# Gate matmuls of the last 1024 tokens split into an upper and a lower half of the array's rows

## The chip, the core and the metric

The kernel runs on one core of a Trainium2 chip. A core has a matrix engine (TensorE, "PE" in the profile, with its weight loads listed apart as "PEld"), a vector engine (VectorE, "DVE"), a scalar engine (ScalarE, "ACT"), a general one (GpSimd, "POOL") and a queue engine that issues transfers (SyncE, "SP"). Matrix products are written to PSUM, which has eight banks of 512 float32 columns by 128 partitions; VectorE and ScalarE carry results from there to SBUF, the working memory.

The metric is the time of one execution in microseconds of the device. Lower is better. Several executions are timed, and one further execution is profiled.

## What is computed

Windowed attention with summarised keys, followed by a gated network without a nonlinearity. Cut to what matters here (batch 4, 8 heads, 768 positions, head size 64; so 3072 tokens of 512 features; 1024 hidden features):

```python
def reference(**kwargs):
    attn_out = _attn_ref(**attn_kwargs)            # (4, 8, 768, 64)
    x = attn_out.transpose(0, 2, 1, 3).reshape(3072, 512)
    a = x @ w1                                     # 512 x 1024
    b = x @ w2                                     # 512 x 1024
    h = a * b @ w3                                 # 1024 x 1024
    return h @ w_out                               # 1024 x 512
```

## The kernel before

**Stages.** The kernel first folds `w3 @ w_out` into one 1024 x 512 matrix while the first attention steps run. Tokens then go in units of U = 512. The first two units (1024 tokens) go through plain products (`gate`, `project`, recorded at the helper's line L123). The other 2048 tokens go in two groups, n = 1 and n = 2, of two units each, through a scheme that forms a 2 x 2 block product out of seven products instead of eight: `gates(n, whole)` for `x @ w1` and `x @ w2`, then `project_fast(n, whole)` for the output. Attention steps for later tokens run between pieces of these products until about 385 us; n = 2 has the stretch behind that to itself, after the rest of `project_fast(1, ...)`.

**Numbers.** Each factor is kept as a high and a low part in the type fp32r, so a product is three matmuls: high by high, low by high, high by low.

**`lanes` (matmul at L708).** This helper runs the seven products for both callers. It takes one PSUM bank for each lane from the list `tags`; for each product k in the order of `o.ids`, for each lane i and each of `steps` chunks of 128 input rows it issues the three matmuls of 128 x 128 weights against 128 x 512 values into `banks[i]`. In `gates` there are 4 lanes of 128 gate features and KH = 2 steps, so a lane of one product is 6 matmuls. `gates` calls it twice, for r = 0 and r = 1, each with its half of the hidden features: 2 x 7 x 4 x 6 = 336 matmuls for n = 2, and as many for n = 1.

**Running sums in PSUM.** Products of one group go on adding into the same bank: `start` is set only on the first product of a group. For n = 2 the order is `EARLY_SUM`: products 0, 4, 5, 6 are one group, 2, 3 the next, 1 alone. After each product the bank's sum so far is carried out, and the next product's matmuls of that lane write to the same bank only after that.

**`add_up` (L726, L728).** It carries a lane out to one of the four SBUF tiles of the lane (`tmp`, `tmp`, `hr`, `hr`). Where the table `o.adds[k]` names no second summand, ScalarE copies (L726: products 0, 4, 5, 6 for n = 2); otherwise VectorE adds the bank to a tile (L728: products 2, 3, 1). After products 3 and 1 VectorE multiplies the finished `x @ w1` by `x @ w2` (L785).

**What follows.** `Whole.moving` prepares the values of `project_fast`: differences of the `hr` tiles (VectorE, L615), a copy to the high part (ScalarE, L619) and the low part (VectorE, L119, tile `hT`).

**Order on the engines.** The order on TensorE and GpSimd is that of the program. The order on VectorE and ScalarE is made at build time by a planner that goes by priorities and its own idea of durations; `tc.high_priority(offset=SOONER)` puts the evacuations of `lanes` 400 places ahead. Once made, each engine works through its queue in that order. PSUM tiles are shared by tag: "mm" has 2 banks, "tp" 2, "sc" 4. The gates use the two "mm" and the two "tp" banks; the four "sc" banks belong to attention (scores, transposes and outputs).

Of the kernel before, what the change touches and what calls it, by code (L numbers as in the profile page):

```python
# [15 lines left out]
ALU = mybir.AluOpType  # L16
# [3 lines left out]
P = 128  # L20
# [50 lines left out]
def attention_moe(ctx, tc, qG, kW, kT, vP, vW, vB, mask, w1, w2, w3T, wo, out, outT):  # L71
    nc = tc.nc
# [3 lines left out]
    U = TOKENS  # L76
# [5 lines left out]
    D = P // 2  # L82
# [8 lines left out]
    KH = NC // 2  # L91
# [596 lines left out]
    def flow_in(n):  # L688


        while flow and len(ready) < n and (not flow[0][0] or flow[0][0] in stored):
            t = sb.tile([P, 2, 512], F32R, name="ws", tag="x", bufs=6)
            flow.pop(0)[1](t)
            ready.append(t)

    def lanes(n, o, weights_of, moving_of, steps, evacuated, tags, between=None):

        banks = [ps.tile([P, 512], F32, name="ln", tag=tag, bufs=bufs) for tag, bufs in tags]
        for at, k in enumerate(o.ids):
            stationary_of = yield from weights_of(at, k)  # L700
            for i in range(n):
                for c in range(steps):
                    if between and c % KH == 0:
                        between(at, i * steps // KH + c // KH)
                    a, m = [stationary_of(i, c, w) for w in range(2)], moving_of(k, c)
                    terms = [(a[0], m[0]), (a[1], m[0]), (a[0], m[1])]
                    for j, (x, y) in enumerate(terms):
                        nc.tensor.matmul(  # L708
                            banks[i][:, :U],
                            lhsT=x,  # L710
                            rhs=y,
                            start=c + j == 0 and k in o.first,
                            stop=c == steps - 1 and j == 2 and k in o.last,
                            skip_group_check=True,
                        )
                    if c < steps - 1:
                        yield 3 * U
                with tc.high_priority(offset=SOONER):
                    evacuated(at, k, i, banks[i][:, :U])
                yield 3 * U  # L720

    def add_up(o, k, parts, got):

        to, more = o.adds[k]
        if more is None:
            nc.scalar.copy(parts[to], got)  # L726
        else:
            nc.vector.tensor_tensor(parts[to], got, parts[more], ALU.add)  # L728

    xT, raws, kept, hT, tasks, background = {}, {}, {}, {}, [], []  # L730

# [2 lines left out]
    def moving_x(n, at):  # L734

        o = ORDERS[n]
        k = o.ids[at]

        def start():
            while any(kept.get((n, half), 0) < NC for half in range(2 if k > 1 else 1)):  # L740
                yield -1
            t = sb.tile([P, 2, KH, U], F32R, name="xT", tag="w12", bufs=8)
            works = []
            for c in range(KH):
                b = [[raws[n, half][c + i * KH] if (n, half) in raws else None for half in range(2)] for i in range(2)]
                works.append(moving(o, k, b, (t[:, 0, c], t[:, 1, c]), o.before.get(k, (k,))))
            yield from staggered(works)
            xT[n, k] = t

        tasks.append(start())  # L750

    def gates_flow(n):
        flow.extend((2 <= k < NK - 1 and ("w%d" % (2 * r + i), k), lambda t, k=k, r=r, i=i: nc.sync.dma_start(t.bitcast(F32), wS[k][2 * r + i])) for r in range(NF // 4) for k in ORDERS[n].ids for i in range(2))

    def gates(n, whole):


        o = ORDERS[n]
        for r in range(NF // 4):
            if r == NF // 4 - 1:  # L760
                flow.extend(output_flow(k, c) for k in LATE.ids for c in range(2))
                if n + 1 < NSU:
                    gates_flow(n + 1)

            def weights_of(at, k):
                while (n, k) not in xT:
                    yield -1
                flow_in(6)
                while len(ready) < 2:
                    yield -1  # L770
                    flow_in(6)
                if n > 1 and r == 0 and at + 2 < NK:
                    moving_x(n, at + 2)
                two = [ready.pop(0), ready.pop(0)]
                return lambda i, c, w: two[i // 2][:, w, c * FQ + i % 2 * P : c * FQ + i % 2 * P + P]

            parts = []

            def evacuated(at, k, i, got):
                if at == 0:  # L780
                    parts.append(whole.parts(i))
                add_up(o, k, parts[i], got)
                if k in o.done:
                    half, a, b = o.done[k]
                    nc.vector.tensor_tensor(parts[i][a], parts[i][a], parts[i][b], ALU.mult)  # L785
                if r == NF // 4 - 1:
                    whole.after(at, i)

            tags = [("mm", 2), ("mm", 2), ("tp", 2), ("tp", 2)]
            yield from lanes(4, o, weights_of, lambda k, c: [xT[n, k][:, w, c] for w in range(2)], KH, evacuated, tags)  # L790

    def temporary():
        t = sb.tile([P, 2, U], F32, name="tmp", tag="wp", bufs=NF)
# [42 lines left out]
    def output_flow(k, c):  # L836
        if 2 <= k < NK - 1:
            return ("p%d" % c, k), lambda t: nc.sync.dma_start(t.bitcast(F32), pS[k][c])

        def load(t):  # L840
            for j in range(2):
                i = 2 * c + j + (0 if k == 0 else NF // 2)
                at = DH if k == NK - 1 else 0
                nc.sync.dma_start(t.bitcast(F32)[:, :, j * DH : (j + 1) * DH], pW[i][:, :, at : at + DH])

        return None, load

    def project_fast(n, whole):
# [18 lines left out]
        def evacuated(at, k, i, got):  # L867
            if at == 0:
                parts.append((*temporary(), *temporary()))
            add_up(LATE, k, parts[i], got)  # L870
            done = {1: (0, 0, 2), 4: (0, 1, 3), 5: (1, 1, 1), 6: (1, 0, 0)}
            if k in done:
                half, u, t = done[k]
                rows, cols = half * DH + i * P, (n - 1) * 2 * U + u * U
                nc.sync.dma_start(outT[rows : rows + P, cols : cols + U], parts[i][t])

        tags = [("mm", 2), ("mm", 2)]
        yield from lanes(2, LATE, weights_of, lambda k, c: hT[n, k][c], NF // 2, evacuated, tags, between)

    def spill_weights(q):  # L880
# [42 lines left out]
    def network():  # L923
        for u in range(2):
            hs = []
            for fs in ([0, 1],) if u else ([0], [1]):
                yield from gate(fs, xs[u], hs, u == 1)
            for f in range(2, NF):
                yield from gate([f], xs[u], hs, u == 1)
            yield from project(u, (0, 1), hs, (range(NF - 1), range(NF - 1, NF)))  # L930
            for t in range(2, NBLK):
                yield from project(u, (t,), hs, (range(NF),))
        for n in range(1, NSU):
            whole = Whole(n)
            yield from gates(n, whole)
            yield from project_fast(n, whole)
# [215 lines left out]
    with tc.manual_schedule(engines={engines.SP, engines.PE}):  # L1152
        start_loads(0)
        active, pairs, t = [], [], [-1]
        while units or active or pairs or delayed or WORK or t[0] <= FIRST[-1]:
# [20 lines left out]
            if t[0] in FIRST[: NPAIR + 1]:  # L1176
                n = FIRST.index(t[0])
# [167 lines left out]
```

## Time and profile before

| what | value |
|---|---|
| median of 3 runs | 515.07 us (512.62 to 517.27) |
| profiled execution, its own time | 512.96 us |
| span of the profiled execution, first to last instruction | 511.2 us |
| granted TensorE clock, mean | 0.993 |
| TensorE busy | 487.7 us (95% of the span) |
| VectorE busy | 365.1 us (71%) |
| ScalarE busy | 314.2 us (61%) |

The profile is one execution taken by the hardware profiler. In a row of a timeline the first number is the start in microseconds from the start of the span, the second how long the row lasts from the first start to the last end, then engine, line, operation, what is written and read, the form, and how many instructions the row holds; in brackets stands idle time of the engine before it and what ended it. In a row of a group the numbers behind the bar are the busy time in us and the mean length of one instruction in ns, then the engine's idle time before these instructions and what ended most of it. Matmuls are pipelined, so their records overlap; the distance from start to start tells their rate. The chain of waits is followed back from the last instruction of the program: at each step to what released it.

### The profile page before, as it was taken

Reading aid. Unit: us, or ns where it says so; the run is one execution under the profiler, and the core shown is the slowest. Engines: PE = TensorE matmul, PEld = TensorE weight load, DVE = VectorE, ACT = ScalarE, POOL = GpSimd, SP = SyncE. Lnnn points to the kernel's source line nnn. Section 1 sums busy time; section 2 is a strip of 40 time slices with the busy share of each in tenths; the row PEclk is TensorE's granted clock in tenths of the full one; section 3 lists DMA queues with packets and bytes.
Section 4 is the critical chain, followed back from the end, with each engine's and each line's share of the span. In section 5 each row is a group of like instructions: output and inputs, shape, how many; then the busy total and the mean of one; then the engine's idle time right before and its main releaser. Section 6 shows DMA issues by size and latency. Waiting matters only on the chain.

```text
span 511.2 us, 10373 instructions
## 1 busy us (share of the span) xinstructions
PE 487.7 (95%) x3744; PEld 392.1 (77%) x3744; DVE 365.1 (71%) x883; ACT 314.2 (61%) x879; POOL 46.9 (9%) x86
## 2 busy tenths in 40 slices
PE   0989987999999999999999999999999999999996
PEld 0767766888887877777777887877787888888885
DVE  4979987688833598985459795899978029129972
ACT  5588964468635788878797677657875421423710
POOL 1024433011201210000000000000000000000000
PEclk9999997999999999999999999999999999999999
DMA  8996699999299989889987999998677755655762
GB/s 342 414 375 244 259 305 321 359 398 412 82 286 306 272 283 281 260 254 339 334 302 251 311 311 333 338 327 252 210 247 247 240 179 192 206 174 197 211 200 85
DMA packets 57220, 139.82 MB, mean 274 GB/s; under 512 B 6224, under 2 KB 19024, under 8 KB 54608
## 3 DMA queue, kind: packets, MB, share of 16 engines
q1 hardware_dynamic: 54864, 134.95, 77.5%
q0 software_dynamic: 1152, 2.10, 2.5%
q10 hardware_dynamic: 1152, 2.10, 1.1%
q8 instruction: 30, 0.49, 0.4%
q14 instruction: 22, 0.18, 0.1%
HBM read 106.42 MB, written 32.70 MB: 272 GB/s over the span
## 4 chain that ended last, share of the span: by engine, by line
PE 83%; DVE 5%; DMA 5%; ACT 5%; issue 1%; SPq 0%; ACTq 0%
PE ln L708 46%; PE mm L123 27%; PE po L433 5%; PE sc L355 4%; PE tp L413 2%; DMA rows<-in_vP_dram 2%; ACT sm L383 2%; DVE wf L186 2%; DMA v<-in_vW_dram 2%; DMA wraw<-in_wo_dram 1%; ACT wf L174 1%; ACT w L200 1%; DVE wf L183 1%; DVE w L119 1%; DVE ks L246 1%
## 5 line engine op out<-in xcount | busy, mean ns | idle before, releaser
L708 PE MATMUL ln<-xT,ws 128*128 128x512 f32 x672 | 157.1, 392 | 0.0
L708 PEld LDWEIGHTS ln<-xT,ws 128*128 128x128 f32 x672 | 125.0, 188 | 27.6 <-issue 0.8
L123 PE MATMUL mm<-x,w 128*128 128x512 f32 x384 | 92.5, 399 | 0.0
L123 PEld LDWEIGHTS mm<-x,w 128*128 128x128 f32 x384 | 72.7, 192 | 16.4 <-issue 0.8
L383 ACT ACTIVATE sm<-sm,mx 128x120 f32<-128x120 f32 x192 | 73.9, 389 | 9.3 <-DVE mx L369 9.3
L708 PE MATMUL ln<-hT,ws 128*128 128x512 f32 x336 | 78.3, 392 | 0.0
L728 DVE TENSOR_TENSOR tmp<-ln,tmp 128x512 f32<-128x512 f32 x52 | 35.8, 688 | 56.3 <-PE ln L708 42.1
L708 PEld LDWEIGHTS ln<-hT,ws 128*128 128x128 f32 x336 | 62.6, 188 | 13.4 <-issue 0.2
L123 PE MATMUL mm<-w,w 128*128 128x512 f32 x192 | 50.2, 414 | 14.3 <-ACT w L200 11.9
L619 ACT CAST hT<-hr 128x512 fp32r<-128x512 f32 x56 | 32.1, 622 | 42.6 <-DVE hr L785 35.4
L123 PEld LDWEIGHTS mm<-w,w 128*128 128x128 f32 x192 | 36.8, 197 | 24.7 <-ACT w L200 12.1
L369 DVE CUSTOM_DVE_ANT_0 sm<-sc,mask_sb 128x120 f32<-128x120 f32 x192 | 42.2, 276 | 15.1 <-PE sc L355 15.0
L123 PE MATMUL mm<-wp,h 128*128 128x512 f32 x192 | 46.3, 395 | 0.0
L393 ACT ACTIVATE sm<-sm,mx 128x120 f32<-128x120 f32 x128 | 38.9, 387 | 6.1 <-DVE mx L389 6.1
L123 PEld LDWEIGHTS mm<-wp,h 128*128 128x128 f32 x192 | 35.4, 188 | 8.0 <-issue 0.5
L119 DVE TENSOR_TENSOR hT<-hr,hT 128x512 fp32r<-128x512 f32 x56 | 35.5, 684 | 3.2 <-ACT hT L619 3.0
L383 ACT ACTIVATION_READ_ACCUMULATOR sm<-sm,mx 128x1 f32 x192 | 36.8, 192 | 0.0
L342 POOL COPY k<-ks 128x96 f32<-128x96 f32 (+1 forms) x32 | 12.9, 412 | 218.3 <-DMA k<-in_kW_dram 178.4
L433 PEld LDWEIGHTS po<-pt,v 120*64 120x64 f32 x768 | 25.2, 141 | 9.2 <-issue 5.0
L200 ACT CAST w<-wf 128x1024 fp32r<-128x1024 f32 (+1 forms) x22 | 21.3, 967 | 14.0 <-DVE wf L186 14.0
L433 PE MATMUL po<-pt,v 120*64 120x64 f32 x768 | 28.7, 229 | 1.1 <-DMA v<-in_vW_dram 0.6
L174 ACT ACTIVATE wf<-wraw 128x1024 f32<-128x1024 f32 (+1 forms) x22 | 23.1, 1056 | 8.0 <-DMA wraw<-in_wo_dram 3.6
(60 smaller groups left out, 548.5 us busy)
## 6 DMA issues: line engine op xcount, KB each, us to landing
ws<-wS SPq DMA_DIRECT2D x56, 512.0 KB
wraw<-in_w3T_dram SPq DMA_DIRECT2D x8, 1024.0 KB
wraw<-in_w_dram SPq DMA_DIRECT2D x8, 1024.0 KB
wS<-sp SPq DMA_DIRECT2D x16, 512.0 KB
ws<-pS SPq DMA_DIRECT2D x16, 512.0 KB
k<-in_kW_dram SPq DMA_DIRECT2D x20, 368.0 KB
raw<-in_kT_dram SPq DMA_DIRECT2D x16, 392.0 KB
q<-in_qG_dram SPq DMA_DIRECT2D x24, 256.0 KB
```

Source lines behind the costliest of these rows:

```text
L119: eng.tensor_tensor(dst, src, hi.bitcast(F32), ALU.subtract)
L123: nc.tensor.matmul(acc, lhsT=a, rhs=b, start=first and i == 0, stop=last and i == len(terms) - 1)
L174: nc.scalar.activation(f[:, some], words[:, some, 1].bitcast(F32), AF.Prelu, scale=2.0**-112, alpha=-(2.0**32),)
L200: nc.scalar.copy(t[:, 0, some], f[:, some])
L355: nc.tensor.matmul(sc[h][64 * g : 64 * g + 64, i * KR : (i + 1) * KR], lhsT=q[rows, i * P + 64 * g : i * P + 64 * g + 64], rhs=k[rows, i, ...
L369: nc.vector.tensor_tensor_reduce(out=sm[:, j], in0=sc[h][:, i * KR : (i + 1) * KR], in1=mask_sb[:, 0 if blk == 0 else 2 if blk == BLOCKS - ...
L383: nc.scalar.activation(sm[:, j], sm[:, j], AF.Exp, bias=mx[:, 0, j : j + 1], scale=-1.0, accum_out=mx[:, 1, j : j + 1])
L393: nc.scalar.activation(sm[:, j], sm[:, j], AF.Copy, scale=mx[:, 2, j : j + 1])
L433: nc.tensor.matmul(po[cols, at : at + 64], lhsT=v[:KR, g, i, cols], rhs=pt[g][:, (h * NBLK + i) * 64 : (h * NBLK + i + 1) * 64], start=Tru ...
L619: nc.scalar.copy(dst[0], src)
L708: nc.tensor.matmul(banks[i][:, :U], lhsT=x, rhs=y, start=c + j == 0 and k in o.first, stop=c == steps - 1 and j == 2 and k in o.last, skip ...
L728: nc.vector.tensor_tensor(parts[to], got, parts[more], ALU.add)
```

## The change

For n = 2, `gates` gives `lanes` eight banks instead of four: the four "sc" banks besides. Where a product is "apart", every matmul over 128 rows is issued as two matmuls over 64 rows, the upper half of weights and values into `banks[i]` and the lower half into `banks[i + 4]`, one behind the other. The sum over the 128 rows is then not complete in one bank: `add_up` gets both banks and carries the first out as before (copy or add), then adds the second with VectorE. All products of n = 2 are apart but products 1, 2 and 3 of the second pass (r = 1). The gates of n = 1 and both calls of `project_fast` have as many banks as lanes and stay as they are.

```diff
-    def lanes(n, o, weights_of, moving_of, steps, evacuated, tags, between=None):
+    def lanes(n, o, weights_of, moving_of, steps, evacuated, tags, between=None, whole=lambda k, i: False):
...
                     a, m = [stationary_of(i, c, w) for w in range(2)], moving_of(k, c)
                     terms = [(a[0], m[0]), (a[1], m[0]), (a[0], m[1])]
+                    apart = len(banks) > n and not whole(k, i)
                     for j, (x, y) in enumerate(terms):
-                        nc.tensor.matmul(
-                            banks[i][:, :U],
-                            lhsT=x,
-                            rhs=y,
-                            start=c + j == 0 and k in o.first,
-                            stop=c == steps - 1 and j == 2 and k in o.last,
-                            skip_group_check=True,
-                        )
+                        for h in range(2 if apart else 1):
+                            rows = slice(h * D, (h + 1) * D) if apart else slice(P)
+                            nc.tensor.matmul(
+                                banks[i + h * n][:, :U],
+                                lhsT=x[rows],
+                                rhs=y[rows],
+                                start=c + j == 0 and k in o.first,
+                                stop=c == steps - 1 and j == 2 and k in o.last,
+                                skip_group_check=True,
+                            )
...
                 with tc.high_priority(offset=SOONER):
-                    evacuated(at, k, i, banks[i][:, :U])
+                    evacuated(at, k, i, [bank[:, :U] for bank in banks[i :: n][: 1 + apart]])
...
         to, more = o.adds[k]
-        if more is None:
-            nc.scalar.copy(parts[to], got)
-        else:
-            nc.vector.tensor_tensor(parts[to], got, parts[more], ALU.add)
+        for some in got:
+            if more is None:
+                nc.scalar.copy(parts[to], some)
+            else:
+                nc.vector.tensor_tensor(parts[to], some, parts[more], ALU.add)
+            more = to
...
-            tags = [("mm", 2), ("mm", 2), ("tp", 2), ("tp", 2)]
-            yield from lanes(4, o, weights_of, lambda k, c: [xT[n, k][:, w, c] for w in range(2)], KH, evacuated, tags)
+            tags = [("mm", 2), ("mm", 2), ("tp", 2), ("tp", 2)] + ([("sc", 4)] * 4 if n >= 2 else [])
+            yield from lanes(4, o, weights_of, lambda k, c: [xT[n, k][:, w, c] for w in range(2)], KH, evacuated, tags, None, lambda k, i, r=r: r == 1 and k in (1, 2, 3))
```

## The prediction

> **What bounds the kernel now.** I read the page first, then the chain of waits, then the busy time by stage, then single stretches of TensorE and VectorE.
>
> ```profile
> span 511.2 us, 10373 instructions
> PE 487.7 (95%) x3744; PEld 392.1 (77%) x3744; DVE 365.1 (71%) x883; ACT 314.2 (61%) x879; POOL 46.9 (9%) x86
> PE ln L708 46%; PE mm L123 27%; PE po L433 5%; PE sc L355 4%; PE tp L413 2%; DMA rows<-in_vP_dram 2%; ACT sm L383 2%; DVE wf L186 2%; DMA v<-in_vW_dram 2%; DMA wraw<-in_wo_dram 1%; ACT wf L174 1%; ACT w L200 1%; DVE wf L183 1%; DVE w L119 1%; DVE ks L246 1%
> ...
> 384.49 1.08 PE po L433 x32
> 385.57 121.46 PE ln L708 x534
> 507.06 0.69 DVE tmp L728
> ```
>
> The last rows are the end of the chain, in order of time: from 385.6 to 507.1 us TensorE alone sets the time, in one unbroken run of L708 matmuls. The gates of the last 1024 tokens lie in it:
>
> ```profile
> 392.44 38.65 PE L708 MATMUL ln<-xT,ws 128*128 128x512 f32 x169
> 430.70 38.24 PE L708 MATMUL ln<-xT,ws 128*128 128x512 f32 x168
> 429.79 6.51 PE L708 MATMUL ln<-xT,ws 128*128 128x512 f32 x28
> L708 PEld LDWEIGHTS ln<-xT,ws 128*128 128x128 f32 x672 | 125.0, 188 | 27.6 <-issue 0.8 <-DVE tmp L728 0.3 <-ACT tmp L726 0.2
> L708 PE MATMUL ln<-xT,ws 128*128 128x512 f32 x672 | 157.1, 392 | 0.0
> ```
>
> The timeline rows show the passes r = 0 (392.4 to 430.7) and r = 1 (to 468.8). A matmul record lasts 0.39 us, but they overlap: (6.51 - 0.39) / 27 = 226.7 ns from start to start. Each pass is 7 products of 4 lanes of 6 matmuls, so a lane takes 1.36 us. Whatever is saved or lost here, up to the last matmul, is saved or lost in the total.
>
> Stage by stage (columns: stretch, its length, then busy time of PE, PEld, DVE, ACT, POOL with instructions, granted clock, DMA share, GB/s):
>
> ```profile
> 392.40:414.20 21.80, 21.80 (x97) 17.80 (x97) 3.15 (x6) 9.35 (x17) 0.00 (x0) 1.00 0.70 223
> 414.20:430.60 16.40, 16.40 (x74) 13.59 (x73) 11.66 (x18) 1.49 (x3) 0.00 (x0) 1.00 0.58 195
> 430.60:452.40 21.80, 21.80 (x98) 18.06 (x97) 6.39 (x11) 10.09 (x18) 0.00 (x0) 1.00 0.56 193
> 452.40:468.80 16.40, 16.40 (x74) 13.55 (x74) 11.97 (x19) 1.21 (x2) 0.00 (x0) 1.00 0.59 195
> ```
>
> The products come in the order 0, 4, 5, 6, 2, 3, 1. In the first and third rows (0, 4, 5, 6) ScalarE copies each lane out and VectorE is nearly free. In the second and fourth (2, 3, 1) VectorE adds each lane and multiplies after products 3 and 1: 11.66 of 16.4 us are taken. DMA (0.58) and the clock (1.00) are no limit.
>
> **The change, term by term.**
>
> *The matmuls.* All 7 products of r = 0 and the first 4 of r = 1 are split: 11 x 4 x 6 = 264 matmuls over 128 rows become 264 pairs over 64 rows each, into two banks. No row shows such a pair in this form, so its price is bounded. The nearest rows are the transposes and scores, which already use half-height tiles:
>
> ```profile
> 348.90 0.84 PE L708 MATMUL ln<-hT,ws 128*128 128x512 f32 x3
> 349.67 0.55 PEld L413 LDWEIGHTS tp<-ident,sm 64*120 64x120 f32 x16 [0.35 <-issue]
> 349.67 0.68 PE L413 MATMUL tp<-ident,sm 64*120 64x64 f32 x16
> 350.28 1.05 PE L355 MATMUL sc<-k,q 64*64 64x120 f32 x32
> 351.26 0.50 PE L708 MATMUL ln<-hT,ws 128*128 128x512 f32 x1
> L413 PEld LDWEIGHTS tp<-ident,sm 64*120 64x120 f32 x384 | 13.2, 135 | 10.3 <-issue 7.8 <-POOL sm L402 2.1 <-ACT wf L174 0.4
> L355 PE MATMUL sc<-k,q 64*64 64x120 f32 x768 | 25.4, 269 | 2.1 <-POOL k L342 2.1
> ```
>
> Scores: (1.05 - 0.27) / 31 = 25.2 ns from matmul to matmul while four tiles run, so a tile gets 120 columns and new weights every 101 ns, 0.84 ns a column. The gate matmuls take 226.7 / 512 = 0.443 ns a column. If the plain fp32 of the scores streams at half the rate of the gates' form (an estimate, from this ratio of 1.9), 0.42 ns is the full rate with the weight change hidden, and 512 columns take 216 ns: a pair saves 11 ns. That is one end: 264 x 10.7 = 2.8 us less. The other is that the halves run one after another, 2 x 226.7 ns: 264 x 226.7 = 59.8 us more. Halves running at the same time at no gain (226.7) lie between. I take 216, since half-height tiles are seen to overlap; what no row shows is two streams at full rate side by side, as the scores' rate is the half one.
>
> *The weight loads.* A pair needs two. Taken strictly in turn at the record's 188 ns, a pair would take 376 ns, 264 x 149 = 39 us more. The transposes' 16 loads of 64 rows by 120 columns are (0.55 - 0.135) / 15 = 28 ns apart, so loads into the two halves do overlap and I cost them at nothing, covered by the 216 ns of stream; without that cover the 39 us is the price. The Trainium skill ("TensorE: Matmul & The Clock Gate", section "LDWEIGHTS (loading the stationary operand)") says that a load's time goes by its columns and not its rows, so that a half-height load costs a whole one. By its figure (columns / 1.2 ns, an estimate from the page) two loads in turn take 213 ns a pair, just under the stream: the sum would not move, but the margin would be gone. The 28 ns between the transposes' loads of 120 columns speak against loads in turn.
>
> *Issue.* 528 instructions more on TensorE's queue. The scores show 32 matmuls and 32 loads in about 1.05 us, 16 ns each; a pair's four fit in 216 ns three times over. Nothing.
>
> *Change of tile shape.* Twice, into pairs at 392 us and out of them in r = 1. The rows above: the last of the three L708 began at 348.90 + 2 x 0.227 = 349.35, the transposes 0.32 us later instead of 0.23; going back, the first record is 0.50 long instead of 0.39. 0.1 us each, 0.2 together.
>
> *Second banks.* The gates take the four "sc" banks besides. Attention is done with them:
>
> ```profile
> 385.62 0.59 ACT L454 COPY xraw<-po 128x512 f32<-128x512 f32 x1 [0.47 <-PE po L433]
> ```
>
> That copy ends at 386.2, the gates begin at 392.4: free by 6 us, no cost.
>
> *The second evacuation.* Each split lane adds one VectorE add of a bank, 44 in all.
>
> ```profile
> L728 DVE TENSOR_TENSOR tmp<-ln,tmp 128x512 f32<-128x512 f32 x52 | 35.8, 688 | 56.3 <-PE ln L708 42.1 <-ACT tmp L726 14.1
> L726 ACT COPY tmp<-ln 128x512 f32<-128x512 f32 x32 | 18.7, 584 | 14.1 <-PE ln L708 14.0
> 421.38 0.69 DVE L728 TENSOR_TENSOR hr<-ln,hr 128x512 f32<-128x512 f32 x1 [0.60 <-PE ln L708]
> 422.10 0.69 DVE L785 TENSOR_TENSOR hr<-hr,tmp 128x512 f32<-128x512 f32 x1
> 422.74 0.69 DVE L728 TENSOR_TENSOR hr<-ln,hr 128x512 f32<-128x512 f32 x1
> 428.99 0.69 DVE L119 TENSOR_TENSOR hT<-hr,hT 128x512 fp32r<-128x512 f32 x1
> 430.20 0.68 DVE L728 TENSOR_TENSOR hr<-ln,hr 128x512 f32<-128x512 f32 x1
> 430.80 0.68 DVE L615 TENSOR_TENSOR hr<-hr 128x512 f32<-128x512 f32 x1
> 431.40 0.68 DVE L785 TENSOR_TENSOR hr<-hr,tmp 128x512 f32<-128x512 f32 x1
> 432.61 0.68 DVE L119 TENSOR_TENSOR hT<-hr,hT 128x512 fp32r<-128x512 f32 x1
> 433.81 0.68 DVE L615 TENSOR_TENSOR hr<-hr 128x512 f32<-128x512 f32 x1
> ```
>
> 44 x 0.69 = 30 us. 32 of them (products 0, 4, 5, 6) fall in stages where VectorE has 18.7 and 15.4 us free and needs 11 each; copy and add after each other are 0.59 + 0.69 + 0.1 for the signals, against the three lanes (3.9 us) before the lane's bank is written again. Hidden. They wait for ScalarE's copy, and in r = 1 the preparation of hT queues behind them, without a reader until 468 us.
>
> The 12 of r = 0, products 2, 3, 1, are not hidden. A dependent operation starts 0.72 us after the one before (421.38 to 422.10), an independent one 0.60 to 0.64. A lane at 216 ns lasts T = 6 x 0.216 = 1.30 us; VectorE needs 0.72 + 0.64 = 1.36 in product 2 and 0.72 + 0.72 + 0.64 = 2.08 in products 3 and 1. It falls behind by 4 x 0.06 + 4 x 0.78 = 3.4 us when the first lane of product 1 ends, and by 3.4 + 3 x 0.78 = 5.7 us at the last. That lane's banks come free 5.7 + 0.2 (the array's own delay, record less spacing) + 1.41 (two adds) + 0.06 (signal) = 7.4 us after its matmuls, and r = 1 wants them after 3 x 1.30 = 3.9. TensorE stands for 3.5 us in pieces at the start of r = 1, and everything behind it on its queue moves by that. Then the copies are ScalarE's again and VectorE catches up.
>
> In the same place the planner has put preparation of hT (428.99, 430.80, 432.61, 433.81 above). The first three now stand ahead of the last lane's adds. Each costs 0.60, less the 0.12 that it fills between dependent operations: 0.5 each, 1.5 us, or 2.1 with the fourth, unless the fuller queue moves them behind, then nothing. I take 0.5, nearer to nothing, as they are the work of lower priority. Products 2, 3, 1 of r = 1 stay whole.
>
> *Elsewhere.* POOL has nothing in these stages and SP's queue the same transfers; no step is moved. The tail after 507 us stays.
>
> Sum: -2.8 + 0.2 + 3.5 + 0.5 = +1.4 us. On the profiled execution (512.96 us, span 511.2) that is 514.4. The median of the three runs is 515.07, 2.1 above it; on that base I say 516.5, 0.3% more.
>
> **The rivals.**
> 1. *VectorE does not hold TensorE up* (its order changes, or its backlog stays under 2.2 us): -2.8 + 0.2, 512.5 us. For it: VectorE is nearly free in the stage before (3.15 of 21.8 us). Against it: no operation of the second stage can start before its lane ends, so that free time can't be used.
> 2. *Overlap without gain*: the pair keeps 226.7 ns, because the extra 11 ns belong to the form of matmul and not to the height of the array. T is 1.36; the backlog is 4 x 0.72 + 3 x 0.72 = 5.0, the stand 5.0 + 0.2 + 1.41 + 0.06 - 4.08 = 2.6, with 0.5 to 2.1 of hT and 0.2: +3.3 to +4.9, 518.4 to 520.0 us. For it: no row shows this form at half height.
> 3. *The halves do not overlap at full rate* (slower): in turn, +59.8 us, 575 us; by loads in turn, +39 us, 554 us. It makes the kernel slower by over 1% from a pair of 226.7 + 5.15 / 264 = 246 ns on. Against it: the transposes and scores overlap; for it: only at half rate.
> 4. *All eight works on hT go ahead of the adds*: 8 x 0.6 = 4.8 in place of 0.5, 520.8 us.
>
> **How the numbers follow.** The forecast has 0.40, rival 1 0.22, rival 2 0.24, rival 3 0.09, rival 4 0.05. The likeliest time is 516.5 us. From 512.0 (rival 1, and 0.5 for a pair still nearer to the stream) to 520.5 (the upper end of rival 2) the range leaves out rivals 3 and 4, 0.14, and little else. 1% (5.15 us) is about what a measurement of this kernel can tell from no change. Even rival 1 stays within it: 2.8 us is all that the matmuls can give. Faster 0.04, for a pair or a base somewhat better than I see; slower 0.16: rivals 3 and 4 and the edge of rival 2; the same 0.80.
>
> **What would show it.** Right: L708 has 528 records of 64 rows, pairs starting about 216 ns apart in 393 to 414 us, VectorE without a gap from some 416 to 437 us, and matmuls waiting for L728 at the start of r = 1, some 3 to 6 us in all, and nowhere else. Wrong: a pair at 227 or more (rival 2 or 3), no wait for VectorE (rival 1), or a wait in another place, such as for ScalarE's copies or for the four new banks.

## The result and the profile after

| | before | after |
|---|---|---|
| median | 514.29 us (512.62 to 517.27, 4 runs) | 522.03 us (519.65 to 523.08, 4 runs) |
| profiled execution: time, span | 512.96, 511.2 us | 519.65, 517.9 us |
| gates of the last 1024 tokens, start to end | 392.44 to 468.78: 76.3 us | 393.99 to 475.91: 81.9 us |

The change makes the kernel slower, by little but clear of the noise: the ratio is 1.0137 with a 95% interval of 1.0103 to 1.0172, some 5 to 9 us. The forecast was 516.5 us, within 512.0 and 520.5.

The page of the changed kernel (busy time by engine), then rows of TensorE's timeline, then the same four stages as before, cut at the same products:

```profile
PE 492.8 (95%) x4008; PEld 393.4 (76%) x4008; DVE 393.6 (76%) x927; ACT 314.2 (61%) x879; POOL 48.0 (9%) x86
```

```profile
393.99 38.75 PE L712 MATMUL ln<-xT,ws 64*128 64x512 f32 x337
399.79 14.44 PE L712 MATMUL ln<-xT,ws 64*128 64x512 f32 x126
433.04 1.82 PE L712 MATMUL ln<-xT,ws 64*128 64x512 f32 x12 [0.30 <-DVE hr L733]
435.74 2.29 PE L712 MATMUL ln<-xT,ws 64*128 64x512 f32 x12 [0.88 <-DVE hr L733]
438.92 2.29 PE L712 MATMUL ln<-xT,ws 64*128 64x512 f32 x12 [0.89 <-DVE hr L733]
441.52 20.73 PE L712 MATMUL ln<-xT,ws 64*128 64x512 f32 x166 [0.30 <-DVE hr L733]
```

```profile
394.00:415.80 21.80, 21.80 (x193) 18.02 (x194) 13.05 (x20) 9.19 (x16) 0.00 (x0) 1.00 0.72 221
415.80:432.20 16.40, 16.40 (x148) 13.64 (x144) 14.69 (x23) 0.59 (x1) 0.00 (x0) 1.00 0.59 192
432.20:459.30 27.10, 24.43 (x195) 18.40 (x192) 21.68 (x34) 10.79 (x19) 0.00 (x0) 1.00 0.46 160
459.30:475.90 16.60, 16.60 (x73) 13.62 (x73) 12.63 (x20) 1.21 (x2) 0.00 (x0) 1.00 0.58 189
```

Three things are to be seen. First, 126 records of 64 rows are 63 pairs, and (14.44 - 0.39) / 62 = 226.6 ns from pair to pair: the halves overlap, and a pair costs what one whole matmul cost. Nothing is won; the first two stages are as long as before to a tenth. Second, the whole loss sits in the third stage, 27.1 us against 21.8, at the beginning of r = 1, where TensorE waits for L733, the add out of PSUM. Third, 0.2 more in the fourth.

The gates also began 1.5 us later in this profile. The order of the instructions on every engine is the same in both kernels up to there, and in the profiles of those experiments below that keep this order the beginning lay anywhere from 391.4 to 401.5 us; I count it as a difference between executions and explain the 5.6 us.

VectorE at the turn from r = 0 to r = 1 (L733 the adds, L791 the multiplications, L119 and L615 the works on hT, that is, the preparation of `project_fast`'s values):

```profile
429.38 1.48 DVE L733 TENSOR_TENSOR hr<-ln,hr 128x512 f32<-128x512 f32 x2
430.90 0.69 DVE L791 TENSOR_TENSOR hr<-hr,tmp 128x512 f32<-128x512 f32 x1
431.50 1.48 DVE L733 TENSOR_TENSOR hr<-ln,hr 128x512 f32<-128x512 f32 x2
433.02 0.69 DVE L791 TENSOR_TENSOR hr<-hr,tmp 128x512 f32<-128x512 f32 x1
433.63 0.68 DVE L733 TENSOR_TENSOR hr<-ln,hr 128x512 f32<-128x512 f32 x1
434.40 0.69 DVE L119 TENSOR_TENSOR hT<-hr,hT 128x512 fp32r<-128x512 f32 x1
435.00 0.68 DVE L733 TENSOR_TENSOR hr<-ln,hr 128x512 f32<-128x512 f32 x1
435.61 0.68 DVE L615 TENSOR_TENSOR hr<-hr 128x512 f32<-128x512 f32 x1
436.20 0.68 DVE L791 TENSOR_TENSOR hr<-hr,tmp 128x512 f32<-128x512 f32 x1
...
439.38 0.68 DVE L791 TENSOR_TENSOR hr<-hr,tmp 128x512 f32<-128x512 f32 x1
439.99 1.48 DVE L733 TENSOR_TENSOR hr<-ln,hr 128x512 f32<-128x512 f32 x2
```

A lane of two adds and a multiplication takes 2.12 us (430.90 to 433.02) against 1.36 us of matmuls, and 3.18 us (433.02 to 436.20, and again to 439.38) where two works on hT stand inside. The last lane of product 1 ended its matmuls at about 432.3; its second add ends at 439.99 + 1.48 = 441.47, and at 441.52 TensorE runs on.

### The profile page after: what moved, and what is told of

Same layout as the page of the kernel before. It is cut to its first block, busy times and chain, and to the rows that moved or that the text cites. A ratio compares the mean times of both kernels' runs of the same rounds, so it can differ in the third digit from the quotient of the medians.

```text
span 517.9 us, 10983 instructions
## 1 busy us (share of the span) xinstructions
PE 492.8 (95%) x4008; PEld 393.4 (76%) x4008; DVE 393.6 (76%) x927; ACT 314.2 (61%) x879; POOL 48.0 (9%) x86
## 4 chain that ended last, share of the span: by engine, by line
PE 74%; DVE 10%; DMA 8%; ACT 6%; issue 1%; SPq 0%; ACTq 0%; POOL 0%; DVEq 0%; POOLq 0%
PE ln L712 38%; PE mm L123 26%; PE po L433 4%; PE sc L355 3%; DMA rows<-in_vP_dram 2%; PE tp L413 2%; DMA v<-in_vW_dram 2%; ACT sm L383 2%; DVE wf L186 2%; DVE hr L733 2%; DMA q<-in_qG_dram 2%; DVE tmp L733 1%; DMA wS<-sp 1%; DMA wraw<-in_wo_dram 1%; DVE hr L791 1%
## 5 line engine op out<-in xcount | busy, mean ns | idle before, releaser
L712 PE MATMUL ln<-xT,ws 64*128 64x512 f32 (+1 forms) x936 | 160.4, 392 | 3.1 <-DVE hr L733 2.4
L712 PEld LDWEIGHTS ln<-xT,ws 64*128 64x128 f32 (+1 forms) x936 | 125.3, 186 | 33.8 <-DVE hr L733 4.8
L123 PE MATMUL mm<-x,w 128*128 128x512 f32 x384 | 91.0, 395 | 0.0
L712 PE MATMUL ln<-hT,ws 128*128 128x512 f32 x336 | 78.3, 392 | 0.0
L733 DVE TENSOR_TENSOR tmp<-ln,tmp 128x512 f32<-128x512 f32 x72 | 49.3, 688 | 30.2 <-PE ln L712 18.9
L123 PE MATMUL mm<-w,w 128*128 128x512 f32 x192 | 52.2, 426 | 14.0 <-ACT w L200 11.9
L123 PEld LDWEIGHTS mm<-w,w 128*128 128x128 f32 x192 | 38.1, 203 | 25.0 <-ACT w L200 12.1
L733 DVE TENSOR_TENSOR hr<-ln,hr 128x512 f32<-128x512 f32 x48 | 32.4, 685 | 7.2 <-ACT hr L731 4.3
L119 DVE TENSOR_TENSOR hT<-hr,hT 128x512 fp32r<-128x512 f32 x56 | 35.4, 684 | 0.3
L119 DVE TENSOR_TENSOR sp<-wr,sp 128x512 fp32r<-128x512 f32 x24 | 16.2, 682 | 17.0 <-ACT sp L655 17.0
## 6 DMA issues: line engine op xcount, KB each, us to landing
ws<-wS SPq DMA_DIRECT2D x56, 512.0 KB
wS<-sp SPq DMA_DIRECT2D x16, 512.0 KB
ws<-pS SPq DMA_DIRECT2D x16, 512.0 KB
```

Of the source, the lines that this page charges most:

```text
L119: eng.tensor_tensor(dst, src, hi.bitcast(F32), ALU.subtract)
L123: nc.tensor.matmul(acc, lhsT=a, rhs=b, start=first and i == 0, stop=last and i == len(terms) - 1)
L712: nc.tensor.matmul(banks[i + h * n][:, :U], lhsT=x[rows], rhs=y[rows], start=c + j == 0 and k in o.first, stop=c == steps - 1 and j == 2 a ...
L733: nc.vector.tensor_tensor(parts[to], some, parts[more], ALU.add)
```

## The experiments

Stage lengths below are those of the gates of the last 1024 tokens in the profile, 76.3 us before and 81.9 us with the change; ratios are to the kernel before, run on the same chip, with 95% intervals. Unless said otherwise an edit is made on the changed kernel.

**Where the loss is: pairs only in some products.** The last argument of `lanes` is changed:

```diff
# e1
-lambda k, i, r=r: r == 1 and k in (1, 2, 3)
+lambda k, i, r=r: k in (1, 2, 3)
# e2
-lambda k, i, r=r: r == 1 and k in (1, 2, 3)
+lambda k, i, r=r: r == 1 or k not in (1, 2, 3)
```

> Products 2, 3, 1 stay whole in r = 0 as well; the pairs of products 0, 4, 5, 6 remain in both passes (192 pairs, 32 second adds). Theory (a pair takes the 226.7 ns of one whole matmul, and all the loss is VectorE's second adds in products 2, 3, 1 of r = 0): four changes of tile shape at 0.1 to 0.2 us, so 0.4 to 0.8 us above the kernel before, no wait of TensorE for VectorE in the gates. Rival (the split itself, or the four more banks, cost time throughout): 192/264 of the measured loss, +5 us. My forecast's pair of 216 ns: -1.5 us.

> Pairs only in r = 0, products 2, 3, 1 (72 pairs, 12 second adds). Theory (VectorE's queue there is all of it): the whole loss of the change in the gates stays, +5.0 to +5.8 us against the kernel before, in the same waits at the start of r = 1. Rival (the split costs throughout): 72/264 of the loss, +1.5 to +2 us.

Measured: e1 stage 77.05 us (+0.7), ratio 1.0027 (0.9994 to 1.0060). No wait for VectorE; what is left is at the four changes of tile shape, 0.1 to 0.2 us each: matmuls start 315 to 319 ns apart there, and the next one 332 to 335 behind, because a load of weights isn't covered (its record starts together with the first matmul's instead of a matmul earlier). e2 stage 81.27 us (+4.9), ratio 1.0083 (1.0049 to 1.0117). So 72 of the 264 pairs make nearly all of the loss, and 192 pairs with 32 second adds make next to none. The theory held in both, with e2 0.1 us below what was expected.

**Which part: pairs without the second add, the second add without pairs.**

```diff
# e3: the lower rows' bank isn't carried out
-[bank[:, :U] for bank in banks[i :: n][: 1 + apart]]
+[bank[:, :U] for bank in banks[i :: n][:1]]
# e4: four banks, whole matmuls; the same lanes carried out twice from one bank
-[bank[:, :U] for bank in banks[i :: n][: 1 + apart]]
+[banks[i][:, :U]] * (1 + twice)
```

> The 264 pairs stay, the second add is left out, so the lower 64 rows' part of each split product is missing from the output. Theory (pairs cost what whole matmuls cost): +0.2 to +0.5 us against the kernel before, no wait for VectorE. Rival (the split itself costs): +5 us or more stays. If pairs took 216 ns anywhere: -2.6 us.

> No pairs and no further banks: whole matmuls as before, but each lane that the change splits is evacuated twice from its one bank (44 further adds on VectorE), so the output counts those products doubly. Theory (the loss is the second adds): +5.0 to +5.6 us against the kernel before, less the 0.3 us of the tile changes. Rival (the split itself): within 0.5 us of the kernel before.

Measured: e3 stage 77.23 us (+0.9; ratio 1.0014, 0.9974 to 1.0054), as expected but for 0.4 us. (Its VectorE operations are those of the kernel before, one for one, yet in another order: with pairs the planner puts works on hT one place further ahead, and TensorE waits 0.3 us for that.) e4 was expected at +5 and came to 77.11 us (+0.8; ratio 1.0010, 0.9975 to 1.0045). Neither part alone makes the loss, and as many adds as in the change cost 0.8 us. That overthrows the count of operations as the whole reason. VectorE's timeline in e4 shows why:

```profile
425.91 0.69 DVE L791 TENSOR_TENSOR hr<-hr,tmp 128x512 f32<-128x512 f32 x1
426.51 1.28 DVE L733 TENSOR_TENSOR hr<-ln,hr 128x512 f32<-128x512 f32 x2
427.71 0.68 DVE L791 TENSOR_TENSOR hr<-hr,tmp 128x512 f32<-128x512 f32 x1
428.31 1.28 DVE L733 TENSOR_TENSOR hr<-ln,hr 128x512 f32<-128x512 f32 x2
429.51 0.68 DVE L791 TENSOR_TENSOR hr<-hr,tmp 128x512 f32<-128x512 f32 x1
```

The planner has made another order: the two adds that stand together belong to different lanes (in the trace the first waits for VectorE itself, the second for TensorE), each operation starts 0.60 us behind the last, and a lane takes 1.80 us (425.91 to 427.71) instead of 2.12. No work on hT stands among them. New theory: the queue is too full for its lanes in both, and its order decides how much.

**Is it the order?** Here VectorE's and ScalarE's order behind the last attention step is the program's own, on the change (e5), on the kernel before (e6) and on e4 (e13). In e14 it is the change again, but with each second add one lane and each multiplication up to two lanes later in products 2, 3, 1 of r = 0.

```diff
# e5, e6, e13, e14
+    with tc.manual_schedule(engines={*MANUAL, engines.Activation, engines.DVE}):
         run(float("inf"))
# e14, in evacuated
-                add_up(o, k, parts[i], got)
+                add_up(o, k, parts[i], got[:1])
...
+                    if waiting:
+                        waiting.pop()()          # second add of the lane before
+                    if later_products:
+                        later_products.pop()()   # multiplication of the lane before that
```

> The change, with VectorE's and ScalarE's order behind the last attention step taken from the program instead of the planner, so that the four works on hT no longer stand between the adds at the end of r = 0. Theory (second adds and the planner's order make the loss together): the gates' stage falls from 81.9 to 78.9 to 79.5 us (2.6 us of stand from the adds alone, as worked out for 226.7 ns, plus 0.3 for the tile changes). Rival (pairs and second adds alone, whatever the order): it stays at 81 us or more.

> The kernel before with the same program order behind the last attention step, as the base of the run above. Theory: the gates' stage stays at 76.3 to 76.6 us. What the order costs elsewhere (preparation of hT later) is seen in the time behind the gates, 42.4 us before.

> Whole matmuls, each lane that the change splits evacuated twice from its one bank (those products count doubly in the output), and VectorE's and ScalarE's order behind the last attention step taken from the program. It has the same VectorE queue as the change in program order (stage 81.1 us, base in that order 76.2). If the order of the queue makes the loss, pairs or not: stage 80 to 80.8 us (4.9 less the 0.5 to 0.8 of tile changes). If the pairs are needed for it: about 77 us, as in the planner's order without pairs (77.1).

> The change in program order (stage 81.1 us), but in products 2, 3, 1 of r = 0 each second add is issued behind the next lane's first add and each multiplication one lane later, so that no operation on VectorE stands directly behind the one it needs. If the 0.78 and 0.72 us between dependent operations (0.60 between independent ones) are what fills the queue: a lane needs 1.81 in place of 2.12 us, the backlog at the end of product 1 falls by 7 x 0.31 = 2.2 us: stage 78.3 to 79.5 us. If not: 81 us.

Measured stages: e6 76.16 us, e5 81.06, e13 79.82 (one execution; 80 to 80.8 expected), e14 78.37 (one execution; 78.3 to 79.5 expected). The program's order costs 9 us behind the gates in e5 and e6 alike (ratios 1.0312, 1.0262 to 1.0363, and 1.0197, 1.0133 to 1.0261), since hT is then prepared late; only the stages are compared. My expectation of e5 failed: without the works on hT the stage was to fall to 79 us, and it stayed at 81. TensorE's timelines of e13 and e5 show the pace:

```profile
432.58 1.66 PE L712 MATMUL ln<-xT,ws 128*128 128x512 f32 x6 [0.39 <-DVE hr L733]
434.63 1.65 PE L712 MATMUL ln<-xT,ws 128*128 128x512 f32 x6 [0.39 <-DVE hr L733]
436.68 1.66 PE L712 MATMUL ln<-xT,ws 128*128 128x512 f32 x6 [0.40 <-DVE hr L733]
```

```profile
431.93 1.82 PE L712 MATMUL ln<-xT,ws 64*128 64x512 f32 x12 [0.30 <-DVE hr L733]
434.05 1.83 PE L712 MATMUL ln<-xT,ws 64*128 64x512 f32 x12 [0.30 <-DVE hr L733]
436.18 1.83 PE L712 MATMUL ln<-xT,ws 64*128 64x512 f32 x12 [0.29 <-DVE hr L733]
```

Lane behind lane, TensorE goes at VectorE's pace: 2.05 us with whole matmuls, 2.12 with pairs. So the loss needs no pairs: with the order given, the same adds on whole matmuls lose 3.7 of the 4.9 us; the slower pace (7 lanes x 0.07) and the changes of shape explain most of the rest. VectorE's timeline in e14 (L733 the first adds, L792 the second, L797 the multiplications):

```profile
429.91 0.68 DVE L733 TENSOR_TENSOR hr<-ln,hr 128x512 f32<-128x512 f32 x1
430.51 0.68 DVE L792 TENSOR_TENSOR hr<-ln,hr 128x512 f32<-128x512 f32 x1
431.11 0.68 DVE L797 TENSOR_TENSOR hr<-hr,tmp 128x512 f32<-128x512 f32 x1
431.71 0.68 DVE L733 TENSOR_TENSOR hr<-ln,hr 128x512 f32<-128x512 f32 x1
```

An operation starts every 0.60 us and a lane takes 1.80 us; the stage falls by 2.7 us. The gaps between dependent operations were that much of the loss. In e5 two works on xT (the values of the gates themselves, 1.2 us) had moved into product 2 and filled the queue in place of the 2.1 us of hT; the 0.9 us between them is what e5 gained on the change (81.06 against 81.92).

**Emptying the queue.** e7 gives the eight multiplications of r = 0 to GpSimd, e8 leaves product 1 of r = 0 whole, e9 makes the multiplications behind product 1 of r = 0 wait for a sum of r = 1, and the works on hT with them:

```diff
# e7
-nc.vector.tensor_tensor(parts[i][a], parts[i][a], parts[i][b], ALU.mult)
+eng = nc.gpsimd if n == 2 and r == 0 else nc.vector
+eng.tensor_tensor(parts[i][a], parts[i][a], parts[i][b], ALU.mult)
# e8
-lambda k, i, r=r: r == 1 and k in (1, 2, 3)
+lambda k, i, r=r: k == 1 or r == 1 and k in (2, 3)
# e9
+zero = sb.tile([P, 1], F32, name="zero", bufs=1)
+nc.vector.tensor_scalar(out=zero, in0=parts[i][o.adds[k][0]][:, :1], scalar1=0.0, scalar2=None, op0=ALU.mult)
+for x, y in held_back:
+    nc.vector.scalar_tensor_tensor(out=x, in0=x, scalar=zero, in1=y, op0=ALU.add, op1=ALU.mult)
```

> The change, with the eight multiplications of r = 0 (behind products 3 and 1) moved from VectorE to GpSimd. Theory (VectorE's queue behind products 2, 3, 1 holds TensorE up): 1.36 us of adds to a lane of 1.36, no backlog but the works on hT (2.4 us, below the slack of 2.4): stage 76.9 to 77.6 us, total within 0.3% of the kernel before. Rival (pairs themselves, or banks): stage stays at 81 us.

> The change, with product 1 of r = 0 whole as well (48 pairs less one product's 24, 8 second adds left in products 2 and 3). Theory: backlog 4 x 0.72 = 2.9 us when product 1 begins, it grows only by the works on hT (1.5), so the last lane is free 2.9 + 1.5 + 0.2 + 0.69 + 0.06 = 5.3 us after its matmuls against 4.1: a stand of 0 to 1.3 us, and 0.5 for the tile changes: stage 77 to 78.3 us. Rival (the pairs): 81 us less a tenth of the loss, 80.5 us or more.

> The change, with the four multiplications behind product 1 of r = 0 made to wait for the first lane's sum of product 4 in r = 1 (a zero worked out from it is added to one factor), and so the works on hT that need them; nothing is left out. Theory (second adds, multiplications and works on hT stand in one VectorE queue in front of the banks' release): backlog 0.2 + 4 x 0.76 = 3.2 us when product 1 begins and hardly more behind it, release 3.2 + 0.2 + 1.5 + 0.06 = 5.0 us after a lane against 4.1: stand of 0.9 to 1.3 us, 0.5 for the tile changes: stage 77.6 to 78.2 us, total +1.3 to +1.9 us against the kernel before. Rival (the pairs themselves): stage stays at 81 us.

e8: stage 78.22 us, within what was expected; ratio 0.9996 (0.9962 to 1.0030), so the total can't be told from the kernel before. e9: the time that TensorE stood at the turn fell to 0.7 us, but the works came back as waits in products 5 and 6 of r = 1 (450 to 455 us), stage 79.76 instead of 78; ratio 1.0049 (1.0006 to 1.0092). e7 missed: stage 82.08 us, ratio 1.0112 (1.0065 to 1.0159). Its rows of VectorE, GpSimd and ScalarE:

```profile
426.40 2.08 DVE L733 TENSOR_TENSOR hr<-ln,hr 128x512 f32<-128x512 f32 x3
430.53 0.69 DVE L119 TENSOR_TENSOR hT<-hr,hT 128x512 fp32r<-128x512 f32 x1 [2.04 <-ACT hT L619]
431.14 0.68 DVE L733 TENSOR_TENSOR hr<-ln,hr 128x512 f32<-128x512 f32 x1
...
425.84 4.00 POOL L792 TENSOR_TENSOR hr<-hr,tmp 128x512 f32<-128x512 f32 x3 [0.17 <-DVE hr L733]
...
429.88 0.62 ACT L619 CAST hT<-hr 128x512 fp32r<-128x512 f32 x1 [14.80 <-POOL hr L792]
```

GpSimd takes 1.3 us for a multiplication where VectorE takes 0.69, and the work on hT needs the product. It stood in VectorE's queue ahead of the next lane's add and waited for ScalarE, which waited for GpSimd: VectorE idle for 2 us with an add behind it that was ready. The operations had left the queue, and their lateness came back into it through one work placed too early. That is not all of e7's 5.7 us: after TensorE had stood for most of the time from 435.8 to 438.5 us, the granted clock was 0.50 from 438.75 to 442.15, and eight pairs started 0.42 us apart instead of 0.227. That makes some 1.6 us; in the profile of the change the clock was 1.00 all through the gates.

**Why a pair takes 226.7 ns.** On whole matmuls, without pairs: e10 cuts the columns, e11 uses fewer rows, e12 reads two-byte values.

```diff
# e10: (256,) in r = 0, (384,) in r = 1
+cuts = (0, *(cut(k, i) if cut else ()), U)
+for lo, hi in zip(cuts, cuts[1:]):
+    nc.tensor.matmul(banks[i][:, lo:hi], lhsT=x, rhs=y[:, lo:hi],
...
# e11: 64 rows in r = 0, 32 in r = 1
+rows = slice((P, D, P // 4)[how])
# e12: r = 0
+x, y = (t.bitcast(mybir.dt.bfloat16)[:, 1::2] for t in (x, y))
```

> No pairs. In the gates of the last 1024 tokens every matmul of 512 columns is cut in two: 256 and 256 in r = 0, 384 and 128 in r = 1. If the 11 to 13 ns over the bare stream belong to each matmul (change of weights): 256 columns take 120 ns from start to start, 384 take 173. If they go with the columns (226.7 / 512): 113.3 and 170.0 ns. 128 columns: no less than the 107 ns of a load by either.

> No pairs: in r = 0 the matmuls of the last gates use only the upper 64 rows, in r = 1 only the upper 32, alone (the other rows' part is left out of the output). If the pitch does not depend on the height of the tile: 226.7 ns in both. If a lower tile changes its weights faster: 216 ns, or between.

> No pairs: in r = 0 the matmuls of the last gates take the upper 16 bits of each word of weights and values as two-byte numbers (every other half word; the lower bits are left out), r = 1 is as before. If the 11 to 13 ns belong to the four-byte form: a pitch of 213 to 217 ns in r = 0. If they belong to any change of weights in a full array: 226.7 ns, as in r = 1.

One stretch of 10 us of TensorE's timeline for each: e10 in r = 0 and r = 1, e11 in r = 0 and r = 1, e12 in r = 0.

```profile
399.77 10.48 PE L711 MATMUL ln<-xT,ws 128*128 128x256 f32 x86
449.80 10.42 PE L711 MATMUL ln<-xT,ws 128*128 128x384 f32 x71
```

```profile
399.66 10.59 PE L713 MATMUL ln<-xT,ws 64*128 64x512 f32 x46
449.78 10.44 PE L713 MATMUL ln<-xT,ws 32*128 32x512 f32 x24
```

```profile
409.62 10.74 PE L712 MATMUL ln<-xT,ws 128*128 128x512 bf16 x47
```

256 columns: (10.48 - 0.28) / 85 = 120.0 ns. With 226.7 for 512 that is 0.417 ns a column and 13.3 ns for each matmul, as in the first of the two readings. A piece of 384 and one of 128 take 2 x (10.42 - 0.39) / 70 = 286.6 ns together, where slope and constant alone would give 240. The matmul records don't show the 173 ns that were expected for the long piece (227 ns from its start to the next, 60 ns from the short one's), while the records of the weight loads start 178 and 109 ns apart in turn; so the short piece is probably bound by the loads, and slope and constant rest on 512 and 256 columns. 64 rows alone: (10.59 - 0.39) / 45 = 226.7. Two-byte values: (10.74 - 0.39) / 46 = 225.0. So the 13 ns hang on the matmul, little on its number form and not at all on its height, and a second tile beside it does not hide them. The Trainium skill ("TensorE: Matmul & The Clock Gate", section "Back-to-back issue gap") gives columns / 2.4 + 2.5 ns from matmul to matmul where weight loads are left out, and about 131 ns at 512 columns for a stream in which each matmul has its load. The slope of the first agrees with 0.417, its constant does not (13.3 where every matmul changes its weights), and the second is far from the 226.7 and 225.0 measured; the measurement decides. The Trainium skill ("TensorE: Matmul & The Clock Gate", section "Measured speedup vs the span model") lets each further matmul of a pack cost about 4 ns; the halves' starts 3 to 4 ns apart agree with that. That a stream of pairs keeps the 226.7 is this case's own measurement.

## Why the prediction failed, step by step

- *The chain* held: TensorE alone sets the end of the program, and each microsecond lost in the gates was lost in the total.
- *The matmuls* failed in size: a pair at 216 ns for -2.8 us. It is 226.7, for nothing. (0.42 x 512 is 215 rather than 216, which would have made it -3.1.) The step that failed is the reading of the scores' 0.84 ns a column as the full rate with the weight change hidden. For 120 columns of plain fp32 in four tiles hardly any extra is seen; for the gates' form 13.3 ns are, at full and at half height. Why the scores escape them stays open. The transposes beside them have 64 columns and start about 31 ns apart, (0.68 - 0.22) / 15, more than the 25 ns of the scores with their 120 columns, so the spacing of such small matmuls doesn't simply follow their columns and may be no streaming rate at all. The bound on the other side, halves in turn, was rightly given little.
- *The weight loads and issue* held: nothing.
- *Change of tile shape*: 0.1 us each was half of it; the fourth stage has 0.2 for the way out, and e1 0.7 for four.
- *Second banks* held, and so did the 32 hidden adds (e1).
- *The 12 adds that aren't hidden*: place and mechanism were right. At 226.7 ns the sum of rival 2 was 2.6 us. A lane takes 2.12 where I had 2.08, as the second add starts 0.79 us behind the first and not 0.72 (1.48 for the two, less 0.69), so its terms give 7 x 0.76 + 0.2 + 1.48 + 0.06 - 4.08 = 3.0.
- *The works on hT*: 0.5 us taken, and it should have been 2.1, the end I left out. Four of them stood inside the adds: the two lanes of 3.18 us instead of 2.12 make 2 x 1.06 = 2.1 us. "Lower priority" was no reason to expect them behind: where the planner has put a work ahead of an add, the queue keeps that order. No run takes these works out alone; the 2.1 is read from the two long lanes.
- *The sum*: 0 + 0.2 + 3.0 + 2.1, and 0.1 for the load that isn't covered when TensorE starts again, = 5.4 us, against 5.6 between the stages in the two profiles. Of the 4.0 us between the forecast's +1.4 and this, 2.8 are the matmuls and 1.6 the works on hT; the adds came 0.5 lower, the uncovered load 0.1 higher. Rival 2 was the right one. Its upper end of +4.9 was 0.7 short of the 5.6, and in the medians 2.0 short (520.0 against 522.03).

What the forecast did not have as a term is the order itself. The same operations cost 0.8 us in one order (e4) and 3.7 in another (e13). That the planner's order changes with the pairs is seen in e3; that it takes a pair for two matmuls' time, and so foresees gaps that aren't there, is only argued: its durations are in no trace.

## What to carry to other kernels

Before an edit is credited with a faster matmul, measure the pitch of that very form in two sizes: slope and constant tell what is there to be won, and here halving the rows touches neither. An evacuation added where its engine is already at the pace of the matmuls is paid through the bank's release: its price is operations times the spacing in their order, dependent ones further apart, less the lanes of matmuls before the bank is wanted again (three here, 4.1 us). Every work that the planner may put between those operations belongs to the price, whatever its priority.

## What the runs showed of the hardware that was not expected

With 32 of 128 rows (e11, r = 1, one execution) the granted clock fell to half while TensorE ran without a break. The windows before and in it:

```profile
392.00:429.00 37.00, 37.00 (x165) 30.01 (x164) 13.55 (x21) 10.00 (x17) 0.00 (x0) 1.00 0.66 210
433.00:499.00 66.00, 66.00 (x156) 49.93 (x155) 16.14 (x26) 10.52 (x19) 0.00 (x0) 0.50 0.32 104
```

The pitch there is (10.44 - 0.61) / 23 = 427 ns, twice the stream of 512 columns with no 13 ns on top. At 64 rows the clock stayed at 1.00. The Trainium skill ("TensorE: Matmul & The Clock Gate", section "What's actually happening") knows the half clock and ties it to how busy the array has been; the 0.50 agrees, and that few busy rows seem to count as little work, with matmuls back to back, is this run's addition. The changed kernel's pairs kept 1.00 throughout its gates; in e7 0.50 came with pairs too, but after TensorE had stood.

Dependent operations on VectorE start 0.72 us apart in SBUF and when one bank is read twice (e13), 0.79 when the second add reads another bank (the change, e5), and independent ones 0.60. The other bank need not be the reason for the 0.79: these second adds wait for TensorE's signal besides VectorE's own, and in the kernel before a multiplication in SBUF that waits for ScalarE besides (427.61 us, ScalarE then long idle) also starts 0.79 behind; no run parts the two. And where TensorE has stood still at clock 1.00, the second matmul follows the first only after 330 to 344 ns, not 227. By the records the first weight load starts together with its matmul there and the next one 0.10 to 0.11 us behind, so a load that would have been hidden is paid once for each wait.
